# Five small reorderings in a hand-scheduled retention and feed-forward kernel

## The chip, the cores and the metric

The kernel runs on one core of a Trainium2 chip, in one launch. The metric is the device time of an execution in microseconds (us). Engines are named as the profile names them: PE is TensorE (PEld its weight loads), DVE is VectorE, ACT is ScalarE, POOL is GpSimd, SP is the queue of SyncE, which here only issues DMAs.

## The reference, cut to what matters

Eight batches of 576 tokens pass through a retention layer (8 heads of 64, a causal decay instead of a softmax) and then through a feed-forward layer with the activation h + sin(a h)^2 / a. All 4608 tokens share the feed-forward weights.

```python
scores = scale * np.matmul(q, k.transpose(0, 1, 3, 2))
Dmat = np.where(rel >= 0, gamma[:, None, None] ** rel[None, :, :], 0.0)
attn = np.matmul(scores * Dmat, v)                 # 8 x 8 x 576 x 64
x = attn.transpose(0, 2, 1, 3).reshape(4608, 512)
h = x @ w_in                                       # 4608 x 2048
s = np.sin(alpha * h)
out = (h + s * s / (alpha + 1e-09)) @ w_out        # 4608 x 512
```

## The kernel before

**Tiling.** The tokens are worked on in nine blocks: blocks 0 to 7 are the first 512 tokens of a batch each, block 8 is the last 64 tokens of all batches. For a batch b, `at[b]` (class Attention, L254) makes the block's input x, transposed; then the block's feed-forward part runs in 16 units of 128 hidden columns each, and a second product with w_out gives the rows of the output.

**Retention.** A batch's 512 tokens are two parts p of 256, each of two groups g of 128 rows. `cast` (L138) multiplies q and k by powers of the decay into 16 bits, and copies v; it takes a list of halves, so that (0,) or (1,) alone is half of the work. q and k are transposed by PE and copied out (`turn` L209, `take` L222, batches 0 and 1) or by a DMA of SP (`crossed` L201, later batches). `scores` (L353) and `masked` (L371, DVE) make the masked scores; `values` (L384) multiplies them by v: first the terms whose rows lie in the other half of PE's rows (False), then those of the same half (True). Between the two the order of PE's rows must be settled: either PE is drained (`change_rows` L234), or, with `relay=A_`, ACT passes a mark when the first ones are done (`told` L248), which the second ones wait for. `outer` (L285) makes the sums of k and v, per group; `evict`, `evict_bank` and `take_sum` (L307 to L323) copy them out of PSUM, `next_sum` (L325, DVE) and `more` (L341, POOL) chain them from group to group, `to_state` (L331) makes the 16-bit state of a group, and `add_states` (L417) multiplies q by the states into the bank of the values. `keep` (L435) copies the result as x.

**Feed-forward.** For a unit fc of block n: `project` (L533, PE, four matmuls of 512 columns, or two halves of 256) into a PSUM bank, `sine` and `square` (L546, L554, mostly ACT), and `product` (L563, DVE), which reads the bank once more and so sets it free. `gemm2(n, u)` (L582) makes a quarter of the sum for 128 rows c of the output, with c and the quarter from `divmod(u, 4)`; `finish` (L576) copies the rows out of the bank (ACT, or DVE if asked) and stores them with two DMAs of SP. From block 2 on the second product is a seven-product form (class Quarters, L610), for which `weigh` (L597, POOL) adds quarters of w_out beforehand.

**PSUM.** There are eight banks: "h0", "h1", "h2" and "op" of one bank each, "m0" and "m1" of two. Whoever opens a tag waits until its last reader is done.

**Order.** Nothing is scheduled by a planner. The body from L746 is written in the order in which each engine gets its work (a manual schedule): every engine works off its own calls in order, and semaphores tie the engines together. So a line moved in the text moves on its own engine's queue alone, against the others of that engine; the mark of a relay stands in ACT's queue, a `crossed`, `load` or `finish` in SP's. L756 to L1271 are written out by hand: batch 0, block 0 with batch 1 and so on up to block 2. From L1286 a loop writes the blocks 3 to 8 in one pattern (`values()`, L1307, is its part for the retention of the next batch); L1452 on is the end.

**The places of the change** are in the hand-written part: the end of block 0's units with batch 1's first scores (L905 to L945), batch 1's second part (L960 to L982), block 0's last quarter with the first units of block 1 (L1018 to L1026), the states of batch 2 among casts for batch 3 (L1056 to L1085), and batch 3's values with batch 4's sums (L1206 to L1231).

Of the kernel before, what the change touches and what calls it, by code (L numbers as in the profile page):

```python
# [18 lines left out]
def kernel(  # L19
# [68 lines left out]
    V, A_, G_ = nc.vector, nc.scalar, nc.gpsimd  # L88
# [8 lines left out]
    def halves(n):  # L97
        return slice(64 * n, 64 * n + 64)

    def copy(eng, d_, s_):  # L100
        if eng is nc.scalar:
            eng.copy(d_, s_)  # L102
        else:
            eng.tensor_copy(d_, s_)  # L104
# [29 lines left out]
    def slot(b, p):  # L134

        return (2 * (b % 2) if b < 4 else 0) + p

    def cast(b, nm, p, eng, ys=(0, 1)):  # L138
        t_ = raw[b, nm, p]
        if (b, nm, p) not in half:  # L140
            if p < 2:
                if nm == "k":
                    d_ = work.tile([P, 16 * D], F16, tag=f"k16{slot(b, p)}", bufs=1, name="k16")
                elif nm == "q":
                    n = order_of_q.index((b, p)) % 3 if b < 5 else 1 - p
                    d_ = work.tile([P, 16 * D], F16, tag=f"q16{n}", bufs=1, name="q16")
                else:
                    d_ = work.tile([P, 16 * D], F16, tag="v16", bufs=4, name="v16")
                d_ = (
                    d_.rearrange("p (h r d) -> p h r d", r=2, d=D)  # L150
                    if nm == "v"
                    else d_.rearrange("p (a r t d) -> p a r t d", a=4, r=2, t=2)
                )
            elif nm == "v":
                d_ = work.tile([P, H, D], F16, tag="vs16", bufs=B // 2, name="vs16")
            else:
                tag, n = ("qks16", 2) if b % 4 == 0 else (f"k16{int(nm == 'q')}", 1)
                d_ = work.tile([P, 4, 2, D], F16, tag=tag, bufs=n, name=nm + "s16")
            half[b, nm, p] = d_
        dst = half[b, nm, p]  # L160
        if p == 2:
            if nm == "v":
                copy(eng, dst.rearrange("p h d -> p (h d)"), t_.rearrange("p h d -> p (h d)"))
            else:
                eng.tensor_tensor(
                    dst.rearrange("p a t d -> p t a d"),
                    t_.rearrange("p (t a) d -> p t a d", t=2),
                    fac_s[nm].rearrange("p (t a) -> p t a", t=2).unsqueeze(3).to_broadcast([P, 2, 4, D]),
                    MULT,
                )  # L170
        elif nm == "v":
            h0, h1 = 4 * ys[0], 4 * ys[-1] + 4
            copy(
                eng,
                dst[:, h0:h1].rearrange("p h r d -> p (h r d)"),
                t_[:, h0:h1].rearrange("p h x -> p (h x)"),
            )
        else:
            a0, a1 = 2 * ys[0], 2 * ys[-1] + 2
            n = 2 * (a1 - a0)  # L180
            return eng.tensor_tensor(  # L181
                dst[:, a0:a1].rearrange("p a r t d -> p t (a r) d"),
                t_.rearrange("p (t a) x -> p t a x", t=2)[:, :, a0:a1].rearrange("p t a (r d) -> p t (a r) d", r=2),
                fac["halved k" if nm == "k" and b >= HALVED else nm]
                .rearrange("p (t x) -> p t x", t=2)[:, :, 2 * a0 : 2 * a1]
                .unsqueeze(3)
                .to_broadcast([P, 2, n, D]),
                MULT,
            )
# [19 lines left out]
    def turn(b, nm, p, tag, ys=(0, 1)):  # L209
        if (b, nm, p) not in trs:  # L210
            trs[b, nm, p] = psum.tile([P, 1024], F16, tag=tag, bufs=1, name="tr")
        tr, x = trs[b, nm, p], half[b, nm, p]
        for a in range(2 * ys[0], 2 * ys[-1] + 2):
            for r in range(2):
                matmul(  # L215
                    tr[:, 256 * a + 128 * r : 256 * a + 128 * r + 128],
                    x[:, a, r].rearrange("p t d -> p (t d)"),
                    ident,
                    start=(a == 0 and r == 0), stop=True, is_transpose=True, skip_group_check=True,
                )  # L220
# [307 lines left out]
    def bank(tag):  # L528
        if tag[0] == "m":
            return psum.tile([P, 2, 512], F32, tag=tag, bufs=1, name="hps")[:, 0]  # L530
        return psum.tile([P, 512], F32, tag=tag, bufs=1, name="hps")

    def project(n, fc, tag, part=None):  # L533

        if n not in gT:
            gT[n] = work.tile([P, 2, FC, 256], F16, tag="gT", bufs=2, name="gT")
        if (n, fc) not in hps_of:
            hps_of[n, fc] = [bank(tag), None]
        cols = PART[part]
        for a in range(KT):  # L540
            matmul(  # L541
                hps_of[n, fc][0][:, cols], w_in16[:, a, fc * P : (fc + 1) * P], xs[n][:, a, cols],
                start=(a == 0 and part != 1), stop=(a == KT - 1), skip_group_check=True,
            )

    def sine(n, fc):  # L546
        hps = hps_of[n, fc][0]
        s_t = work.tile([P, 512], F16, tag="s", bufs=4, name="s_t")
        nc.scalar.activation(  # L549
            s_t, hps, mybir.ActivationFunctionType.Sin, bias=0.0, scale=alpha_t[:, fc : fc + 1],  # L550
        )
        hps_of[n, fc][1] = s_t
# [10 lines left out]
    def product(n, fc):  # L563
        hps, ss_t = hps_of.pop((n, fc))
        nc.vector.scalar_tensor_tensor(  # L565
            gT[n][:, :, fc, :], ss_t.rearrange("p (t n) -> p t n", t=2), inva[:, fc : fc + 1],
            hps.rearrange("p (t n) -> p t n", t=2), MULT, ADD,
        )
# [7 lines left out]
    def finish(n, c, eng=None, cols=slice(0, 512), issue=(nc.sync, nc.sync)):  # L576
        osb = work.tile([P, 512], F32, tag="osb", bufs=4, name="osb")
        copy(eng or nc.scalar, osb[:, cols], ops[n, c, cols.start][:, cols])
        for r in range(2):
            issue[r].dma_start(rows_of(n, c)[r, :, cols], osb[halves(r), cols])  # L580

    def gemm2(n, u, tag, cols=slice(0, 512)):  # L582
        c, part = divmod(u, 4)
        if (n, c, cols.start) not in ops:
            ops[n, c, cols.start] = psum.tile([P, 512], F32, tag=tag, bufs=1, name="ops")
        for fk in range(4 * part, 4 * part + 4):
            matmul(  # L587
                ops[n, c, cols.start][:, cols], gT[n][:, c // 2, fk, c % 2 * P : c % 2 * P + P], w_out16[:, fk, cols],
                start=(fk == 0), stop=(fk == FC - 1), skip_group_check=True,
            )  # L590
# [102 lines left out]
    at = [Attention(b) for b in range(B)]  # L693
# [52 lines left out]
    with tc.manual_schedule():  # L746
# [159 lines left out]
        sine(0, 14)  # L906
        square(0, 14, A_)
        product(0, 13)
        project(0, 15, "m0")
        sine(0, 15)  # L910
        square(0, 15, A_)
        gemm2(0, 4, "op")
        turn(1, "k", 0, "m1")
        take(1, "k", 0, V, (0,))
        take(1, "k", 0, V, (1,))
        product(0, 14)
        product(0, 15)
        gemm2(0, 12, "h2")
        gemm2(0, 0, "h0")
        turn(1, "q", 0, "m1")  # L920
        take(1, "q", 0, A_, (0,))
        take(1, "q", 0, A_, (1,))
        at[0].to_state(3, G_)
# [13 lines left out]
        load(2, "q", 1)  # L937
        gemm2(0, 1, "h0")
        cast(1, "k", 1, G_)
        at[1].outer((0,), "m0")  # L940
        at[1].evict((0,), A_)
        at[1].to_state(0, G_)
        gemm2(0, 8, "h1")
        at[1].values(0, False, "m1", relay=A_)
        cast(1, "q", 1, V)  # L945
        gemm2(0, 9, "h1")
# [18 lines left out]
        gemm2(0, 2, "h0")  # L965
        gemm2(0, 10, "h1")
        gemm2(0, 15, "h2")
        at[1].outer((1,), "m0")
        at[1].next_sum(2)
        at[1].to_state(2, V)  # L970
        at[1].take_sum(3, A_)
        at[1].values(1, False, "m1", relay=A_)
        gemm2(0, 7, "op")
        finish(0, 3)
        at[1].values(1, True)
        at[1].add_states(1)
        at[1].keep(1, A_)
        finish(0, 1)
        cast(2, "k", 1, V)
        cast(2, "k", 0, V)  # L980
        crossed(2, 0, "k")
        crossed(2, 1, "k")  # L982
# [37 lines left out]
        project(1, 4, "op")  # L1020
        sine(1, 4)
        square(1, 4, A_)
        product(1, 3)
        gemm2(0, 11, "h1")
        finish(0, 2, V)
        project(1, 5, "m0")  # L1026
        product(1, 4)
        sine(1, 5)
# [33 lines left out]
        at[2].more(2)  # L1062
        product(1, 10)
        cast(3, "k", 1, G_, (0,))
        at[2].to_state(2, G_)
        at[2].scores(0, 0, "m0")
        gemm2(1, 0, "op")
        sine(1, 9)
# [11 lines left out]
        square(1, 12, A_)  # L1080
        product(1, 12)
        cast(3, "q", 1, G_)
        project(1, 13, "h1", 0)
        project(1, 13, "h1", 1)
        gemm2(1, 2, "op")  # L1085
# [120 lines left out]
        product(2, 4)  # L1206
        cast(4, "q", 0, G_, (0,))
        finish(1, 2)
        at[4].outer((0, 1), "op", "h0")
        cast(4, "q", 0, G_, (1,))  # L1210
        sine(2, 8)
        weigh(4, 1, G_)
        sine(2, 6)
        at[4].evict_bank(1, A_)
        square(2, 8, V)
        product(2, 8)
# [3 lines left out]
        at[4].to_state(0, G_)  # L1220
        at[4].more(1)
        at[4].more(2)
        at[3].values(0, False, "m1")
        at[3].values(1, False, "m0")
        at[3].values(1, True)
        at[3].add_states(1)
        at[3].keep(1, A_)
# [285 lines left out]
```

## Time and profile before

| what | us |
|---|---|
| median of 3 runs | 295.06 (294.48 to 295.23) |
| the profiled execution | 295.11 |
| its span, first to last instruction | 293.4 |
| PE busy in the span | 281.2 |
| DVE busy | 218.2 |
| ACT busy | 211.0 |
| POOL busy | 209.0 |

A row of a timeline has the start in us from the span's start, the length in us, the engine, the line of the kernel, the operation, what it writes and reads, the shape, and how many neighbouring instructions of this kind it holds; in brackets stands how long the engine had been idle before it, and what ended that. Gaps under 0.15 us are not shown as idle. The ends of matmuls are modelled, so rows of PE overlap a little: the time from one start to the next is what a group takes of PE. A row of windows has the stretch, its length, and each engine's busy time with its count of instructions (PE, PEld, DVE, ACT, POOL), then the granted clock of PE as a share of the full one, the share of the DMA engines and GB/s.

### The profile page before, as it was taken

The numbers are of one execution on the slowest core, as the hardware profiler recorded it, in microseconds if no ns is written. First come the engines' busy times: TensorE is split into PE (matmuls) and PEld (weight loads), VectorE is DVE, ScalarE is ACT, GpSimd is POOL, SyncE is SP. The second block draws the span as 40 slices with busy tenths as digits, with TensorE's granted clock in tenths as the row PEclk, the third lists the DMA queues.
The fourth block names the chain that finished last, engine by engine and source line by source line (L and its number), as shares of the span: only waits on it lengthen the run. The fifth ranks groups of instructions, "written<-read, shape, count | busy, mean of one in ns | idle before, by whom it ended". The sixth has DMA issues, their size and how long they took to land.

```text
span 293.4 us, 8769 instructions
## 1 busy us (share of the span) xinstructions
PE 281.2 (96%) x3611; PEld 184.5 (63%) x3611; DVE 218.2 (74%) x298; ACT 211.0 (72%) x343; POOL 209.0 (71%) x198
## 2 busy tenths in 40 slices
PE   7699899999999999999999999999999999999993
PEld 5474455576644666666666666666666667665782
DVE  3759856999866989988676877687777595747861
ACT  2859733975949898878787878787778879888600
POOL 4888867999999999999998799679916700460000
PEclk9999999999999999999999999999999999999999
DMA  7999999899998787978698795978666101311225
GB/s 227 292 251 222 277 242 303 219 185 300 238 219 274 104 186 180 253 169 199 154 269 179 174 231 143 105 159 188 128 136 152 38 3 39 72 38 30 58 47 118
DMA packets 119159, 49.89 MB, mean 170 GB/s; under 512 B 69824, under 2 KB 118096, under 8 KB 119120
## 3 DMA queue, kind: packets, MB, share of 16 engines
q1 hardware_dynamic: 114528, 45.04, 65.2%
q0 software_dynamic: 4224, 4.19, 8.6%
q8 instruction: 28, 0.46, 0.6%
q10 hardware_dynamic: 368, 0.11, 0.2%
q14 instruction: 11, 0.09, 0.1%
HBM read 36.74 MB, written 9.44 MB: 157 GB/s over the span
## 4 chain that ended last, share of the span: by engine, by line
PE 81%; POOL 7%; DVE 4%; issue 2%; ACT 2%; DMA 2%; DVEq 0%; ACTq 0%; POOLq 0%
PE hps L541 35%; PE hps L658 29%; PE ops L587 7%; PE sc L363 2%; POOL T L608 2%; PE o L406 2%; DVE gT L565 2%; DMA qT<-q 2%; PE idle L702 1%; PE kv L298 1%; DVE ret L375 1%; PE tr L215 1%; POOL kvs L345 1%; POOL q L181 1%; POOL v L104 1%
## 5 line engine op out<-in xcount | busy, mean ns | idle before, releaser
L565 DVE SCALAR_TENSOR_TENSOR gT<-ss_t,inva,hps 128x512 f16<-128x512 f16 x144 | 105.0, 742 | 39.5 <-ACT ss_t L558 37.5
L549 ACT ACTIVATE s_t<-hps,alpha_t 128x512 f16<-128x512 f32 x144 | 96.5, 681 | 37.4 <-PE hps L541 37.0
L541 PE MATMUL hps<-xT,w_in 128*128 128x512 f16 (+1 forms) x604 | 121.3, 347 | 1.3 <-DVE gT L565 1.2
L541 PEld LDWEIGHTS <-w_in 128*128 128x128 f16 x668 | 63.5, 98 | 51.7 <-issue 1.6
L558 ACT ACTIVATE ss_t<-s_t 128x512 f16<-128x512 f16 x121 | 75.7, 630 | 3.4
L658 PEld LDWEIGHTS <-gT 128*128 128x128 f16 x656 | 63.8, 98 | 14.5
L630 POOL TENSOR_TENSOR gT<-gT,d 128x1024 f16<-128x1024 f16 x12 | 25.3, 2122 | 26.4 <-PE hps L658 25.7
L658 PE MATMUL hps<-T,gT 128*128 128x256 f16 x336 | 39.8, 273 | 0.0
L375 DVE TENSOR_TENSOR ret<-sc,mask 128x1024 f16<-128x1024 f32 (+1 forms) x32 | 35.1, 1117 | 5.0 <-PE sc L363 5.0
L658 PE MATMUL hps<-w_out,gT 128*128 128x256 f16 x320 | 38.2, 273 | 0.0
L678 DVE TENSOR_TENSOR osb<-osb,hps 128x512 f32<-128x512 f32 x35 | 23.9, 683 | 12.8 <-PE hps L658 11.8
L587 PE MATMUL ops<-w_out,gT 128*128 128x512 f16 x128 | 31.0, 380 | 0.0
L181 POOL TENSOR_TENSOR q<-q,cn 128x1024 f16<-128x1024 f32 (+1 forms) x16 | 25.6, 1612 | 0.1
L636 POOL TENSOR_TENSOR gT<-gT 128x1024 f16<-128x1024 f16 x12 | 25.3, 2124 | 0.0
L345 POOL TENSOR_TENSOR kvs<-s,kvs 128x256 f32<-128x256 f32 x23 | 19.3, 839 | 1.8
L332 POOL TENSOR_TENSOR s<-kvs,cn 128x256 f16<-128x256 f32 x22 | 15.4, 700 | 6.2 <-ACT kvs L102 5.4
L587 PEld LDWEIGHTS <-gT 128*128 128x128 f16 x128 | 11.7, 98 | 12.2 <-DVE gT L565 0.2
L181 POOL TENSOR_TENSOR k<-k,cn 128x1024 f16<-128x1024 f32 (+1 forms) x11 | 19.2, 1748 | 0.0
L102 ACT COPY osb<-hps 128x512 f32<-128x512 f32 (+2 forms) x15 | 8.2, 549 | 13.4 <-PE hps L658 13.2
L344 POOL TENSOR_TENSOR s<-kvs,cn 128x256 f32<-128x256 f32 x23 | 16.1, 698 | 1.6 <-DVE kvs L327 1.5
L102 ACT CAST xT<-o 128x1024 f16<-128x1024 f32 (+1 forms) x14 | 13.8, 989 | 4.5 <-PE o L428 4.5
L102 ACT COPY kvs<-kv 128x512 f32<-128x512 f32 (+2 forms) x15 | 8.1, 546 | 9.6 <-DVE kvs L327 5.0
(78 smaller groups left out, 279.1 us busy)
## 6 DMA issues: line engine op xcount, KB each, us to landing
out_dram<-osb SPq DMA_DIRECT2D x70, 128.0 KB, 2.6
q<-in_q_dram SPq DMA_DIRECT2D x16, 512.0 KB, 5.8
k<-in_k_dram SPq DMA_DIRECT2D x10, 512.0 KB, 6.0
v<-in_v_dram SPq DMA_DIRECT2D x10, 512.0 KB, 6.2
k<-in_k_dram SPq DMA_DIRECT2D x24, 128.0 KB, 3.5
v<-in_v_dram SPq DMA_DIRECT2D x24, 128.0 KB, 3.2
w_in<-in_moe_w_in_dram POOLq DMA_DIRECT2D x4, 512.0 KB, 9.1
w_out<-in_moe_w_out_dram POOLq DMA_DIRECT2D x4, 512.0 KB, 9.3
```

Of the source, the lines that this page charges most:

```text
L102: eng.copy(d_, s_)
L181: return eng.tensor_tensor(dst[:, a0:a1].rearrange("p a r t d -> p t (a r) d"), t_.rearrange("p (t a) x -> p t a x", t=2)[:, :, a0:a1].rea ...
L375: made = nc.vector.tensor_tensor(ret.rearrange("p t (z x) -> p (t z) x", z=2)[:, :, 0:n], sc.rearrange("p t (z x) -> p (t z) x", z=2)[:, : ...
L541: matmul(hps_of[n, fc][0][:, cols], w_in16[:, a, fc * P : (fc + 1) * P], xs[n][:, a, cols], start=(a == 0 and part != 1), stop=(a == KT - ...
L549: nc.scalar.activation(s_t, hps, mybir.ActivationFunctionType.Sin, bias=0.0, scale=alpha_t[:, fc : fc + 1],)
L558: nc.scalar.activation(ss_t, s_t, mybir.ActivationFunctionType.Square)
L565: nc.vector.scalar_tensor_tensor(gT[n][:, :, fc, :], ss_t.rearrange("p (t n) -> p t n", t=2), inva[:, fc : fc + 1], hps.rearrange("p (t n) ...
L587: matmul(ops[n, c, cols.start][:, cols], gT[n][:, c // 2, fk, c % 2 * P : c % 2 * P + P], w_out16[:, fk, cols], start=(fk == 0), stop=(fk ...
L630: eng.tensor_tensor(self.part(0, 0, i), self.part(1, 1, i), self.d3[:, 4 * i : 4 * i + 4], SUB)
L636: eng.tensor_tensor(out_, self.part(1, 0, i), self.part(0, 0, i), SUB)
L658: matmul(self.ps[name][:, 256 * m + cols.start : 256 * m + cols.stop], left(j)[:, P * m : P * m + P], right(j)[:, cols], start=(tag is not ...
L678: nc.vector.tensor_tensor(out_, a, self.ps[ps], ADD)
```

## The change

Five groups of lines move; the arithmetic and the number of instructions stay nearly the same.

1. Unit 15 of block 0 is projected into bank "m1" instead of "m0", and the turns of batch 1's first k and q go into "m0" instead of "m1".
2. `gemm2(0, 8)` moves ahead of batch 1's first sums (`outer`), which now stand on PE right before the values of the same part.
3. `finish(0, 3)` moves ahead of batch 1's second sums. The cast of batch 2's second k on DVE, one instruction before, becomes two halves: the first goes ahead of those sums, the second stays. `finish(0, 2)`, the copy of DVE and its store, moves ahead of the product of unit 3.
4. The state of batch 2's group 2 moves behind the cast of batch 3's second q, on POOL.
5. The values of batch 3 of the first kind (False) move ahead of batch 4's sums, and get `relay=A_`: marks on ACT in place of the drain of PE.

```diff
-        project(0, 15, "m0")
+        project(0, 15, "m1")
...
-        turn(1, "k", 0, "m1")
+        turn(1, "k", 0, "m0")
...
-        turn(1, "q", 0, "m1")
+        turn(1, "q", 0, "m0")
...
+        gemm2(0, 8, "h1")
         at[1].outer((0,), "m0")
         at[1].evict((0,), A_)
         at[1].to_state(0, G_)
-        gemm2(0, 8, "h1")
         at[1].values(0, False, "m1", relay=A_)
...
         gemm2(0, 15, "h2")
+        finish(0, 3)
+        cast(2, "k", 1, V, (0,))
         at[1].outer((1,), "m0")
...
         gemm2(0, 7, "op")
-        finish(0, 3)
         at[1].values(1, True)
         at[1].add_states(1)
         at[1].keep(1, A_)
         finish(0, 1)
-        cast(2, "k", 1, V)
+        cast(2, "k", 1, V, (1,))
         cast(2, "k", 0, V)
...
-        product(1, 3)
         gemm2(0, 11, "h1")
         finish(0, 2, V)
+        product(1, 3)
         project(1, 5, "m0")
...
-        at[2].to_state(2, G_)
         at[2].scores(0, 0, "m0")
...
         cast(3, "q", 1, G_)
+        at[2].to_state(2, G_)
...
-        at[4].outer((0, 1), "op", "h0")
         cast(4, "q", 0, G_, (1,))
         sine(2, 8)
         weigh(4, 1, G_)
         sine(2, 6)
+        at[3].values(0, False, "m1", relay=A_)
+        at[3].values(1, False, "m0", relay=A_)
+        at[4].outer((0, 1), "op", "h0")
         at[4].evict_bank(1, A_)
...
-        at[3].values(0, False, "m1")
-        at[3].values(1, False, "m0")
         at[3].values(1, True)
```

## The prediction, made before the changed kernel ran

> **What bounds the kernel now.** I read the head of the page, then busy time by stage, then the timeline of each engine where the diff works.
>
> ```profile
> span 293.4 us, 8769 instructions
> PE 281.2 (96%) x3611; PEld 184.5 (63%) x3611; DVE 218.2 (74%) x298; ACT 211.0 (72%) x343; POOL 209.0 (71%) x198
> ```
>
> ```profile
> 31.00:79.50 48.50, 46.31 (x749) 28.27 (x751) 40.67 (x53) 31.06 (x51) 43.80 (x43) 1.00 1.09 248
> 79.50:286.00 206.50, 206.30 (x2476) 137.20 (x2476) 155.64 (x213) 158.95 (x253) 143.18 (x118) 1.00 0.62 141
> ```
>
> The first number after the length is TensorE's busy time. Nearly all of the diff lies in 31 to 79.5 us, where TensorE idles 2.19 us; from 79.5 to 286 it idles 0.20 us. So a lead that TensorE gains early should reach the end, unless another engine gives out on the way. The sum of removable idle time is small, 0.75% of the span. I follow one quantity, TensorE's lead over the profiled execution, from edit to edit. That execution took 295.11 us (span 293.4 and 1.71 around it); the median is 295.06.
>
> **Unit 15 in other banks.**
>
> ```profile
> 31.89 1.02 PE L541 MATMUL hps<-xT,w_in 128*128 128x512 f16 x4 [0.86 <-DVE gT L565]
> 32.75 1.03 PE L587 MATMUL ops<-w_out,gT 128*128 128x512 f16 x4
> 31.76 0.73 DVE L565 SCALAR_TENSOR_TENSOR gT<-ss_t,inva,hps 128x512 f16<-128x512 f16 x1
> ```
>
> Unit 15 waits until unit 10's product frees bank m0. Bank m1, last used by unit 4, is free, so this wait goes. What is late next is gemm2(0, 4): its bank "op" is freed by the product of unit 11, the third row, which ends at 32.49. It can start at 32.55 instead of 32.75: **lead 0.20**, not 0.86. The turns now stand in m0, free by then; the scores that use m0 next wait for the copies of q, which they read anyway, instead of unit 15's product.
>
> **Batch 1's sums next to its values.**
>
> ```profile
> 39.80 0.45 PE L298 MATMUL kv<-v,k 64*64 64x64 f16 x32
> 41.15 0.42 PE L406 MATMUL o<-ret,v 64*64 64x128 f16 x16
> 41.49 1.04 PE L587 MATMUL ops<-w_out,gT 128*128 128x512 f16 x4
> 39.66 1.21 DVE L375 TENSOR_TENSOR ret<-sc,mask 128x1024 f16<-128x1024 f32 x1
> ```
>
> Before, the sums wait for a mask, then four full matmuls run, then the values. After, the four go first, cover the wait, and the two groups of 64x64 tiles stand together. The values still need the second mask, which ends at 40.87, now 40.67: start 40.73 instead of 41.15. The way into small tiles is then already paid (0.07 of the 0.34 between the second and third row is my estimate; between 0 and 0.1 little hangs on it), so gemm2(0, 9) starts at 41.00: **lead 0.49**. The sums' eviction and the state, which come later than TensorE's lead alone would make them, are read only behind four more full matmuls, a turn and the second half of the values.
>
> **Half a cast and a store in idle time.**
>
> ```profile
> 46.12 2.36 DVE L375 TENSOR_TENSOR ret<-sc,mask 128x1024 f16<-128x1024 f32 x2 [0.54 <-PE sc L363]
> 49.52 0.86 DVE L327 SCALAR_TENSOR_TENSOR kvs<-kvs,cn,kv 128x64 f32<-128x64 f32 x4 [1.05 <-PE kv L298]
> 50.76 3.30 DVE L181 TENSOR_TENSOR k<-k,cn 128x1024 f16<-128x1024 f32 x2
> 30.50 0.68 DVE L181 TENSOR_TENSOR k<-k,cn 128x512 f16<-128x512 f32 x1
> 94.33 1.36 DVE L181 TENSOR_TENSOR k<-k,cn 128x512 f16<-128x512 f32 x1
> 93.10 2.05 POOL L181 TENSOR_TENSOR q<-q,cn 128x512 f16<-128x512 f32 x2
> 47.84 1.16 POOL L608 TENSOR_TENSOR T<-w_out 128x512 f16<-128x512 f16 x1
> 50.47 0.37 ACT L102 COPY kvs<-kv 128x256 f32<-128x256 f32 x1 [5.02 <-DVE kvs L327]
> ```
>
> VectorE idles 1.05 us before the chained sum. Half a cast costs 0.68 (fourth row) to 1.36 (fifth; GpSimd's casts in the sixth run until 95.15, and 0.68 before the fifth ends is 95.01): it may not fit. Here GpSimd works on a weight sum until 49.00 (47.84+1.16), about 48.8 with the lead of 0.2 that it inherits. If the half cast runs only behind that, it ends near 49.35, and the chained sum, due at 49.03, is 0.22 late. Behind it stand ACT's take_sum and, in ACT's queue behind that, the mark that releases TensorE's second values: TensorE's lead falls by about as much, to 0.3. I take this; with room for the half cast it would stay 0.49.
>
> From the Trainium skill, "SBUF — State Buffer", Practical consequences: a VectorE instruction with two SBUF inputs contends with a GpSimd instruction that reads SBUF, and whoever issued first holds the port for its whole length. The fifth row agrees (1.36 against 0.68): its half cast runs only behind GpSimd's. By this rule the half cast is late as above, and so is a state further down; with no such lock the sum would end near 1.2 of lead ahead of batch 3's scores instead of 0.9.
>
> In exchange, of the 3.30 us of two casts only one and a half remain, with less waiting between the engines: VectorE comes out of them about 0.8 sooner (0.68 to 1.3 saved, less the late sum). The store of rows 3 moves ACT's copy and two DMA issues of SP from behind the take_sum at 50.47 to where ACT idled (5.02); SP's queue, which holds the transposes further down, gets past these two issues sooner.
>
> **The store of rows 2 ahead of a product.**
>
> ```profile
> 58.88 1.05 PE L541 MATMUL hps<-xT,w_in 128*128 128x256 f16 x8 [0.34 <-DVE gT L565]
> 60.14 0.72 PE L298 MATMUL kv<-v,k 64*64 64x64 f16 x64 [0.21 <-DVE osb L104]
> 58.08 1.40 DVE L565 SCALAR_TENSOR_TENSOR gT<-ss_t,inva,hps 128x512 f16<-128x512 f16 x2
> 59.40 0.68 DVE L104 COPY osb<-ops 128x512 f32<-128x512 f32 x1
> ```
>
> TensorE waits here twice, for the first of the two products and for the copy. VectorE's lead of 0.8 carries to the first product. TensorE arrives 0.3 sooner and can give up the 0.34 of idle time and some 0.15 that its pipeline loses around it, 0.8 too: it starts near 58.1. The copy moves one product (about 0.66) ahead, so the second wait disappears: batch 2's sums start near 59.07, **lead 1.07**. The displaced product, 0.7 later than it could be, frees a bank that is asked for only behind the sums, whose row is 0.72 long.
>
> **Batch 3's q ahead of a state.**
>
> ```profile
> 72.45 0.61 POOL L332 TENSOR_TENSOR s<-kvs,cn 128x256 f16<-128x256 f32 x1
> 73.02 1.90 POOL L181 TENSOR_TENSOR q<-q,cn 128x1024 f16<-128x1024 f32 x1
> 74.21 1.26 DVE L181 TENSOR_TENSOR k<-k,cn 128x512 f16<-128x512 f32 x1
> 72.77 1.47 SPq L205 DMA_TRANSPOSE kT<-k  x1
> 74.95 1.23 SPq L205 DMA_TRANSPOSE qT<-q  x1
> 74.98 0.51 PE L428 MATMUL o<-qT,s 64*64 64x128 f16 x24
> 79.46 0.42 PE L363 MATMUL sc<-qT,kT 64*64 64x128 f16 x16 [0.41 <-DMA qT<-q]
> ```
>
> GpSimd works with hardly a gap here (43.80 of 48.50 us above), so it keeps what it gains once: 0.2 (the lead it inherits) to 0.8 (with half a cast less to wait for), of which I take 0.78. The cast of q gains another 0.57, the state's place: it ends at 73.57 instead of 74.92. The state comes behind it, and behind VectorE's half cast (third row), which by then waits for GpSimd too: it starts near 74.0 and ends near 74.6. Its reader, the last third of the 24 matmuls, stood near 75.2 and could come at 74.1: it now waits 0.5, and the lead falls to 0.53.
>
> At the scores TensorE had lost some 0.54 (0.41 idle, the rest an estimate of what its pipeline adds), so without that wait the lead would be 1.07. How far the landing, just before 79.46, moves no row shows. Bounds: not at all (the DMA queue as full as before), or by the cast's 1.35. SP must first issue k's transpose (1.47), and the stores and casts that it waits for come 0.5 to 0.8 sooner; between these and 1.35 I take 0.9: **lead 0.9** at 79.5.
>
> **Values ahead of batch 4's sums.**
>
> ```profile
> 97.45 0.71 PE L298 MATMUL kv<-v,k 64*64 64x64 f16 x64
> 99.61 0.60 PE L541 MATMUL hps<-xT,w_in 128*128 128x512 f16 x2
> 98.28 0.58 ACT L102 COPY kvs<-kv 128x512 f32<-128x512 f32 x1
> 101.56 0.69 ACT L549 ACTIVATE s_t<-hps,alpha_t 128x512 f16<-128x512 f32 x1 [0.19 <-PE hps L541]
> 126.34 0.64 PE L406 MATMUL o<-ret,v 64*64 64x128 f16 x32
> 128.33 1.04 PE L541 MATMUL hps<-xT,w_in 128*128 128x512 f16 x4
> 127.80 0.58 ACT L102 COPY kvs<-kv 128x512 f32<-128x512 f32 x1 [0.29 <-PE kv L298]
> 108.47 0.75 DVE L565 SCALAR_TENSOR_TENSOR gT<-ss_t,inva,hps 128x512 f16<-128x512 f16 x1 [0.46 <-ACT ss_t L558]
> 108.33 1.97 PE L541 MATMUL hps<-xT,w_in 128*128 128x512 f16 x8
> ```
>
> ```profile
> 101.50:108.50 7.00, 6.78 (x12) 1.00 0.75 168
> ```
>
> The window is of ACT alone.
>
> The new order, with marks on ACT in place of TensorE's drain, is that of batch 4 at 126.34. There the group takes 1.99 (126.34 to 128.33); here 2.16 (97.45 to 99.61): 0.17 saved on TensorE. But the eviction by ACT starts 1.46 behind the group's start there (127.80), here 0.83 (98.28): **0.63 later**. Queued behind it on ACT are a square, the second eviction, a keep and the sines. ACT has 0.28 of room before 101.56 (0.19 idle, and the 0.09 by which neighbours overlap) and from there works without a gap (6.78 of 7.00 us in the window above) to the square that releases the product at 108.47. That product ends at 109.22, and the second four of the eight matmuls at 108.33 start at 109.27 (their end, 110.30, less the 1.03 that four take): they wait for it already. So 0.63-0.28 = **0.35 of the lead is lost**. Between 0.18 late (if the sums end as long after their start as before) and 0.17 gained (if ACT had room that I don't see), I take 0.35, since the row of batch 4 is the same order of work. GpSimd's lead of 0.7 is enough for what follows.
>
> **Sum.** 0.9-0.35 = 0.55: 295.11-0.55 = 294.56, by the median **294.5 us**.
>
> **The rivals.**
> 1. *The early gain passes whole.* q lands with its cast, and ACT has room at 98: 1.07+0.17 = 1.24, so 293.8. For it: TensorE is the only engine without gaps. Against it: ACT's unbroken row to 108.47. Chance 0.28.
> 2. *Late sums on ACT, and nothing kept.* The transposed q lands just before 79.46 as before, because the DMA queue sets it and not the cast; the scores give back every early gain, and ACT's late eviction costs 0.35: 295.4, slower than before. It decides as soon as the landing moves by less than 0.35. For it: from q's issue at 74.95 to the scores at 79.46 stand 4.5 us, over three times the issue itself. Chance 0.10.
> 3. *The half cast isn't hidden.* It delays the chained sum by its full 0.7 and VectorE gains nothing; the waits at 58.88 and 60.14 keep all but the moved copy. At the scores only the cast's 0.57 counts: 0.57-0.35 = 0.2, so 294.85. Chance 0.15.
>
> **How the numbers follow.** The forecast, 294.2 to 294.8 by its own bounds, has 0.47. The range reaches to rivals 1 and 2: 293.7 to 295.4. A measurement of this kernel tells about 0.3% (0.89 us) from no change: faster means below 294.2. Rival 1 and the forecast's edge give 0.35; slower than 295.9 needs rival 2 with a further loss, 0.06; the rest, 0.59, is within.
>
> **What would show it.** Right: unit 15 without a wait and gemm2(0, 4) near 32.55; sums and values side by side near 40.3; no wait for a copy ahead of batch 2's sums, which start near 59.1; a wait inside the 24 matmuls near 74.1; scores near 78.6 instead of 79.46; ACT's first eviction of batch 4 1.4 behind the values, and a longer wait for the product that was at 108.47. Wrong: scores still at 79.46 (the DMA queue), no longer wait there (ACT's room), or a new wait between 80 and 97, where I find none.

## The result, and the profile after

| kernel | median, us | runs | ratio to the kernel before, 95% |
|---|---|---|---|
| changed, first measurement | 295.12 (294.10 to 296.63) | 14 | 1.0002 [0.9982, 1.0021] |
| changed, again (`e8`) | 294.46 (293.91 to 296.68) | 12 | 0.9981 [0.9955, 1.0008] |

Forecast were 294.5 and "within 0.3%"; that it is, both times. But the first time nothing at all was gained over the kernel before, whose 14 runs beside it have a median of 295.03. The 26 runs together have a median of 294.6. The 14 runs of the first measurement fall in two groups, six from 294.10 to 294.34 and eight from 295.05 to 296.63. The profiled execution of the first measurement took 296.25, that of the second 294.68, with the same program. So two traces of one kernel can be compared, and they tell more than before against after. Further down, one slow run each of `e1` (298.39), `e9` (366.10) and `e10` (298.31) counts in the median and not in the ratio.

One part of the spread is there without the change too. Three of the eight longer runs (295.61, 295.75, 296.63) had a mean granted clock of TensorE of 0.992 to 0.994. The kernel before has such runs too: those at 0.994 or less have medians of 295.6 to 295.9 on the three chips, the others of 294.6 to 294.8. One profile caught such a run, that of `e7` below (296.13, clock 0.993). Its windows show a lower clock near the start (third number from the end), and TensorE begins its first projection at 18.70 us, where it was 17.52 before:

```profile
10.00:15.00 5.00, 3.62 (x42) 2.26 (x42) 4.45 (x5) 4.15 (x11) 4.34 (x6) 0.87 1.21 259
15.00:20.00 5.00, 4.54 (x147) 3.54 (x146) 2.83 (x5) 1.54 (x4) 3.96 (x7) 0.79 1.24 222
```

The two profiles of the changed kernel have no such stretch; what sets them apart is something else.

The page of the changed kernel, first measurement, and its windows for the two stretches of the prediction:

```profile
span 294.5 us, 8771 instructions
PE 280.7 (95%) x3611; PEld 184.3 (63%) x3611; DVE 217.1 (74%) x299; ACT 211.3 (72%) x343; POOL 207.9 (71%) x198
...
q8 instruction: 28, 0.46, 0.7%
```

```profile
31.00:79.50 48.50, 45.57 (x744) 28.30 (x742) 40.43 (x53) 31.39 (x52) 43.63 (x43) 1.00 1.08 244
79.50:286.00 206.50, 205.62 (x2466) 136.46 (x2466) 154.07 (x212) 158.26 (x251) 142.19 (x118) 1.00 0.63 142
```

TensorE idles 2.93 us in the first stretch, where before it was 2.19. The timeline of TensorE, changed kernel, first measurement:

```profile
32.35 1.02 PE L587 MATMUL ops<-w_out,gT 128*128 128x512 f16 x4 [0.66 <-DVE gT L565]
...
58.87 0.71 PE L298 MATMUL kv<-v,k 64*64 64x64 f16 x64
...
62.45 0.42 PE L363 MATMUL sc<-qT,kT 64*64 64x128 f16 x16 [1.01 <-DMA qT<-q]
...
80.16 0.42 PE L363 MATMUL sc<-qT,kT 64*64 64x128 f16 x16 [1.50 <-DMA qT<-q]
```

The same view of the second measurement:

```profile
32.55 0.81 PE L587 MATMUL ops<-w_out,gT 128*128 128x512 f16 x3 [0.66 <-DVE gT L565]
...
40.25 0.45 PE L298 MATMUL kv<-v,k 64*64 64x64 f16 x32
40.72 0.42 PE L406 MATMUL o<-ret,v 64*64 64x128 f16 x16
41.07 0.39 PE L587 MATMUL ops<-w_out,gT 128*128 128x512 f16 x1
...
59.07 0.71 PE L298 MATMUL kv<-v,k 64*64 64x64 f16 x64
...
61.56 0.42 PE L363 MATMUL sc<-qT,kT 64*64 64x128 f16 x16
...
74.61 0.31 PE L428 MATMUL o<-qT,s 64*64 64x128 f16 x8 [0.17 <-POOL s L332]
...
78.40 0.42 PE L363 MATMUL sc<-qT,kT 64*64 64x128 f16 x16
```

Up to batch 2's sums both are the same, but for 0.20 by which the first execution was ahead before any edit acts (58.87 and 59.07). Then the first one waits 1.01 us at scores(2, 0, 1) and 1.50 at scores(3, 1, 1), for a transposed q; the second doesn't wait at the first, and at the other for 0.23 only. That small wait stands with TensorE's weight loads, so the row above doesn't show it; the chain that ended last names the transfer:

```profile
78.40 0.25 PEld L363 LDWEIGHTS <-kT 64*64 64x64 f16 x15 [0.23 <-issue]
```

```profile
73.57 4.75 DMA qT<-q
78.32 0.08 issue
78.40 0.42 PE sc L363 x16
```

That is where the gain goes: not off the path, but into waits for a transfer that comes in time in one execution and late in another.

Why late? SP's timeline, first measurement, then the second:

```profile
47.55 2.22 SPq L121 DMA_DIRECT2D q<-in_q_dram  x1
49.82 4.82 SPq L580 DMA_DIRECT2D out_dram<-osb  x4
54.75 2.75 SPq L205 DMA_TRANSPOSE kT<-k  x2
57.60 1.25 SPq L205 DMA_TRANSPOSE qT<-q  x1
```

```profile
47.63 1.68 SPq L121 DMA_DIRECT2D q<-in_q_dram  x1
49.36 4.25 SPq L580 DMA_DIRECT2D out_dram<-osb  x4
53.72 2.73 SPq L205 DMA_TRANSPOSE kT<-k  x2
56.56 1.25 SPq L205 DMA_TRANSPOSE qT<-q  x1
```

On VectorE the casts of k end at 53.05 (first) and 53.25 (second), that of q at 55.79 and 55.99, so the issue isn't late for them. One load and four stores take SP 7.0 us in the first measurement, 5.9 in the second: the issue itself is held up (the first store alone 2.89 against 1.82), and q's transpose goes out 1.04 later. It then meets something. Windows of one microsecond, first measurement (the last two columns are the share of the DMA engines, by the packets that start in the window, and GB/s):

```profile
58.00:59.00 1.00, 1.00 (x24) 0.72 (x26) 1.00 (x3) 0.97 (x3) 1.00 (x2) 1.00 0.84 180
59.00:60.00 1.00, 1.00 (x69) 0.91 (x66) 1.00 (x3) 1.00 (x2) 1.00 (x2) 1.00 2.71 93
60.00:61.00 1.00, 1.00 (x12) 0.89 (x10) 1.00 (x3) 0.67 (x2) 1.00 (x2) 1.00 0.04 5
61.00:62.00 1.00, 0.44 (x5) 0.14 (x2) 1.00 (x2) 0.52 (x1) 1.00 (x1) 1.00 0.77 162
```

The DMA view of the first measurement from 58.8 to 59.3:

```profile
q1 hardware_dynamic: 458, 0.12, 177.0%
q8 instruction: 1, 0.02, 20.5%
```

A share of 2.71 with 93 GB/s means that packets which start in this microsecond run on past its end; in the next, 5 GB/s move. One packet of 16 KB of the queue "instruction" stands right before the standstill. It is read here as a fetch of code, by its pace TensorE's (the page counts 28 for 2 x 3611 rows of PE and PEld, one for 258). In the second measurement the fetch comes at 59.0 too, but the transposes have landed:

```profile
59.00:60.00 1.00, 1.00 (x69) 0.86 (x68) 1.00 (x3) 0.97 (x2) 1.00 (x1) 1.00 0.42 73
60.00:61.00 1.00, 1.00 (x11) 0.90 (x10) 1.00 (x2) 0.86 (x2) 1.00 (x2) 1.00 0.80 229
```

### The profile page after: what moved, and what is told of

Read it like the earlier page. It is cut to its first block, busy times and chain, and to the rows that moved or that the text cites. A ratio compares the mean times of both kernels' runs of the same rounds, so it can differ in the third digit from the quotient of the medians.

```text
span 294.5 us, 8771 instructions
## 1 busy us (share of the span) xinstructions
PE 280.7 (95%) x3611; PEld 184.3 (63%) x3611; DVE 217.1 (74%) x299; ACT 211.3 (72%) x343; POOL 207.9 (71%) x198
## 4 chain that ended last, share of the span: by engine, by line
PE 75%; POOL 7%; DVE 6%; DMA 4%; ACT 3%; issue 2%; SPq 1%; ACTq 0%; POOLq 0%
PE hps L541 32%; PE hps L658 29%; PE ops L587 6%; DVE gT L565 2%; POOL T L608 2%; PE o L406 2%; PE sc L363 2%; DMA k<-in_k_dram 2%; DVE ret L375 2%; DMA qT<-q 2%; DVE k L181 2%; ACT s_t L549 1%; SPq L121 1%; POOL q L181 1%; PE kv L298 1%
## 5 line engine op out<-in xcount | busy, mean ns | idle before, releaser
L332 POOL TENSOR_TENSOR s<-kvs,cn 128x256 f16<-128x256 f32 x22 | 14.6, 664 | 8.2 <-ACT kvs L102 7.4
L345 POOL TENSOR_TENSOR kvs<-s,kvs 128x256 f32<-128x256 f32 x23 | 18.7, 812 | 1.8
L344 POOL TENSOR_TENSOR s<-kvs,cn 128x256 f32<-128x256 f32 x23 | 15.5, 673 | 1.6 <-DVE kvs L327 1.4
L541 PE MATMUL hps<-xS,w_in 128*128 128x512 f16 x64 | 15.0, 379 | 0.0
```

Of the source, the lines that this page charges most:

```text
L541: matmul(hps_of[n, fc][0][:, cols], w_in16[:, a, fc * P : (fc + 1) * P], xs[n][:, a, cols], start=(a == 0 and part != 1), stop=(a == KT - ...
```

## The experiments

The theory: **TensorE's lead arrives, and is spent at two scores** that wait for transposes; these land late when SP issues them late and a fetch of code stops them in flight. Against it: the lead is lost elsewhere, or to part 5. The first four kernels are `e1` (the changed kernel) and `e2` (the kernel before) with 17 fewer filler matmuls at the start, which makes 34 fewer instructions with their weight loads, so that fetches of code fall later in the work, `e3`, the changed kernel without part 5 (its lines of the diff taken back), and `e4`, the kernel before with these lines alone. For `e1` and `e2`:

```diff
-        keep_busy(16, "h0", 256)
+        keep_busy(8, "h0", 512)
...
-        keep_busy(14, "op", 64)
+        keep_busy(7, "op", 256)
...
-        keep_busy(4, "h1", 256)
+        keep_busy(2, "h1", 512)
```

> The changed kernel; 17 fewer of the matmuls that only keep TensorE warm in the first 14 us (wider ones in their place, the same warm time), so 34 fewer TensorE instructions ahead of all the rest. Theory A: TensorE loads its instructions by a DMA every 256 instructions; one such load (58.9 us in the changed profile) falls on the transposes of batch 2's q, another (76.5) on those of batch 3's q, and freezes them for 1.5 to 2 us, so TensorE waits at batch 2's and batch 3's scores and gives its early lead of about 1.07 back. 34 instructions later the two loads fall some 3 us later, on transposes nobody waits for: no wait before batch 2's scores, at most a few tenths before batch 3's, time about 294.0, 1 us below the changed kernel, and less spread. Theory B (SP's earlier store fills the DMA queue and makes the transposes late): same as the changed kernel, 295.1. Theory C (only the values ahead of the sums cost): also 295.1.

Measured 295.18 (ratio 0.9998 [0.9978, 1.0018]): **no gain, a miss.** The trace did what was meant: the fetch moves from 58.9 to 62.5, scores(2, 0, 1) doesn't wait, and the standstill is now there, on a transpose that nobody waits for (windows of `e1`):

```profile
59.00:60.00 1.00, 1.00 (x69) 0.77 (x67) 1.00 (x2) 0.97 (x3) 1.00 (x2) 1.00 0.50 73
...
63.00:64.00 1.00, 1.00 (x12) 0.89 (x10) 1.00 (x2) 1.00 (x3) 1.00 (x2) 1.00 1.99 72
```

But scores(3, 1, 1) waits 0.38. One place eased is not enough. And the run tells less than it was made for: q's transpose also went out 0.66 earlier than in the first measurement (56.94), and the new filler isn't free. The first projection begins at 17.89 in this profile and at 18.26 in that of `e2`, while at a full clock it is 17.20 to 17.52 in all the others.

> The kernel before, with the same 34 fewer TensorE instructions at the start. Theory A: the load at 76.5, which freezes the transposes of batch 3's q for 1.4 us, moves away and the wait of 0.4 to 0.5 us before batch 3's scores goes: about 294.6, if no other load falls on a transpose in its place. Theories B and C: no change, 295.0.

Measured 295.09 (1.0000 [0.9984, 1.0016]): as the kernel before; no wait at scores(3, 1, 1) in its profile.

> The changed kernel with its fifth part undone (values of batch 3 behind batch 4's sums, TensorE drained). Theory C, from the changed profile: 0.3 less than the changed kernel, since ACT's first eviction of batch 4 starts 0.6 sooner: about 294.8; unit 3's projection of block 3 waits less. If the fifth part costs nothing: as the changed kernel, 295.1, or 0.17 more.

Measured 294.98 (1.0003 [0.9984, 1.0022]): 0.14 under the changed kernel's first measurement, which these runs can't tell from nothing. Its profiled execution is one of the good ones (293.99): no wait at either scores.

> The kernel before with the fifth part alone. Theory C: 0.3 slower than before, 295.35, all of it lost between the values at 97.5 and the projection at 109.3. If ACT has room: 0.17 faster, 294.85.

Measured 294.91 (1.0005 [0.9991, 1.0019]). In the trace TensorE's lead falls from 0.92 to 0.54 over part 5, but the execution stayed about 0.5 ahead (0.32 of it from before any edit acts); the median does not show a loss.

Changes of single places, timed by their medians, settled little. For `e3` the clock is one reason: eight of its twelve runs are at 0.994 or less, in `e1` one, in `e2` none. The second four give TensorE other work ahead of the two scores. `e5` is the changed kernel with both moved, `e6` the same without part 5, `e7` the kernel before with scores(3, 1, 1) moved, `e8` the changed kernel as it is:

```diff
-        at[2].scores(0, 1, "m0")
         product(1, 6)
-        at[2].masked(0, 1)
...
         project(1, 9, "h2", 1)
+        at[2].scores(0, 1, "m0")
+        at[2].masked(0, 1)
...
-        at[3].scores(1, 1, "m0")
         at[3].evict((0, 1), A_)
-        at[3].masked(1, 1)
         product(2, 3)
         gemm2(1, 7, "h0")
         gemm2(1, 3, "op")
+        at[3].scores(1, 1, "m0")
+        at[3].masked(1, 1)
```

> The changed kernel with two scores moved to where TensorE has other work in front of them: scores(2, 0, 1) and its mask behind project(1, 9), 0.87 us later; scores(3, 1, 1) and its mask behind gemm2(1, 7) and gemm2(1, 3), 1.73 us later and next to scores(3, 1, 0). Theory (TensorE's early lead is given back at these two scores, which wait for transposes that land when the DMA queues let them): the two waits (1.01 and 1.50 us in the changed kernel's profile, 0 to 0.38 in the first two looks at relatives of it) are gone or under 0.3, and the time falls to 293.7 to 294.0, with less spread from run to run. First rival (the lead is lost elsewhere, the waits only show it): another wait takes their place before 110 us, and the time stays at 295.1. Second rival (only the neighbours of equal tile size count): 0.3 less from the saved change of tile size, 294.8, and the spread stays.

Measured **293.99** (0.9968 [0.9945, 0.9992]), no run over 294.97. The profiled execution shows the theory's core best, since it had the late issue (q's transpose at 58.15) and the standstill, and didn't wait. (It is the second longest of the twelve all the same: the eight full matmuls behind batch 3's sums take 2.19 us, from 78.16, where they take 1.83 in `e10`, and the trace names nothing that they wait for.) Its windows and its timeline of TensorE:

```profile
59.00:60.00 1.00, 1.00 (x68) 0.91 (x68) 1.00 (x3) 1.00 (x2) 1.00 (x2) 1.00 2.40 153
60.00:61.00 1.00, 1.00 (x12) 0.90 (x10) 1.00 (x2) 0.81 (x2) 1.00 (x1) 1.00 0.13 5
```

```profile
62.54 0.42 PE L363 MATMUL sc<-qT,kT 64*64 64x128 f16 x16
```

> The kernel of the first run with the values of batch 3 back behind batch 4's sums, as before the change. Theory: ScalarE's late eviction (0.31 to 0.38 us lost in the profiles) is the second place of loss, and it counts once TensorE has a lead to lose: 0.3 less than the first run, 293.4 to 293.7. Rival (what ScalarE gives is taken by the product behind it anyway): the same as the first run.

Measured 293.80 (0.9959 [0.9934, 0.9985]), 0.19 under `e5`: a smaller step than expected.

> The kernel before with scores(3, 1, 1) and its mask alone moved, 1.73 us later. It waited 0.41 us there in the profile and nothing in two later looks. Theory: 0.3 from the saved change of tile size and 0 to 0.4 from the wait, 294.2 to 294.5. Rival (this place costs the kernel before nothing): 294.8 to 295.0, as before.

Measured 294.64 (0.9991 [0.9967, 1.0015]), 0.23 under the kernel before on this chip (294.87). By size it lies between theory and rival; it doesn't decide. Its trace is against one half of the theory: from batch 3's sums to the matmul behind the last scores TensorE takes 3.10 us, in `e2`, with the scores apart and no wait, 3.11. So the saved change of tile size is not the 0.3 that was expected.

> The changed kernel itself, to stand beside the three others on one chip. Theory: 295.1, in two groups of runs, one near 294.2 and one at 295.1 to 296.6, as the waits at the two scores fall. Rival (the two groups were chance): one group near 295.1.

Measured 294.46; eleven of twelve runs lie from 293.91 to 294.90, without the gap of the first measurement. **Neither side held:** the shares of good and bad executions differ from one time to the next. None of these twelve is at a clock of 0.994 or less.

The last four ask whether the issue order on SP is to blame, and where the rest of the lead goes. `e9` is the changed kernel with q0's transpose ahead of k1's, `e10` is `e9` with scores(3, 1, 1) later as in `e5`, `e11` is `e10` without part 5, and `e12` is the changed kernel with finish(0, 3) back in its old place:

```diff
         crossed(2, 0, "k")
-        crossed(2, 1, "k")
...
         crossed(2, 0, "q")
+        crossed(2, 1, "k")
...
         gemm2(0, 15, "h2")
-        finish(0, 3)
...
         gemm2(0, 7, "op")
+        finish(0, 3)
```

> The changed kernel with one line moved: on SP, the transpose of batch 2's first q is issued ahead of the transpose of its second k (order k0, q0, k1, q1 in place of k0, k1, q0, q1). Theory (scores(2, 0, 1) waits in those executions in which SP is blocked in earlier loads and stores, issues q0 from 57.6 on and has it frozen by the instruction fetch at 59): q0 is issued from 55.8 to 56.3 on, as soon as its cast on VectorE ends, lands before 59, and the wait at scores(2, 0, 1) is gone; scores(3, 1, 1) still waits in some executions; 294.0 to 294.4, against 294.46 and 295.12 of the two looks at the changed kernel. Rival (the flow of all transfers sets the landing, whatever the order): the wait stays at up to 1 us, 294.5 to 295.1.

Measured 295.11 (0.9998 [0.9983, 1.0013]): **a miss in time, though the wait at scores(2, 0, 1) is gone** as expected (q issued at 55.98). The lead goes on to the next place. SP and TensorE in `e9`:

```profile
74.11 3.17 SPq L205 DMA_TRANSPOSE qT<-q  x1
```

```profile
79.32 0.42 PE L363 MATMUL sc<-qT,kT 64*64 64x128 f16 x16 [1.12 <-DMA qT<-q]
```

The issue of batch 3's q takes 3.17 us where it took 1.23 before.

> The same, and scores(3, 1, 1) moved 1.73 us later, next to scores(3, 1, 0), as in the fifth run; scores(2, 0, 1) stays where the change has it (the fifth and sixth run lost 0.29 behind it, because the two scores that share bank m0 came too close). Theory: no wait at either scores, 0.3 from the saved change of tile size, nothing lost between 62 and 66: 293.6 to 293.8, below the fifth run's 293.99. Rival (the places of scores are not what is left): 294.0 or more.

Measured **293.97** (0.9970 [0.9955, 0.9985]), 1.14 under `e9`, from which it differs by the place of scores(3, 1, 1) alone. Both scores of the part now stand together, and none waits:

```profile
79.74 0.64 PE L363 MATMUL sc<-qT,kT 64*64 64x128 f16 x32
```

Nearly all of the 1.14 is the wait, 1.12 in the profile of `e9`. The saved change of tile size is worth about 0.1, as the profiles without a wait show: from batch 3's sums to the matmul behind the last scores it is 3.13 us in `e3` (first two rows), with the scores apart, and 3.04 here.

```profile
77.56 0.71 PE L298 MATMUL kv<-v,k 64*64 64x64 f16 x64
80.69 2.76 PE L541 MATMUL hps<-xT,w_in 128*128 128x512 f16 x12
```

```profile
77.27 0.71 PE L298 MATMUL kv<-v,k 64*64 64x64 f16 x64
80.31 2.76 PE L541 MATMUL hps<-xT,w_in 128*128 128x512 f16 x12
```

This median is 0.2 to 0.4 above the expected 293.6 to 293.8, and just under the 294.0 of the rival.

> The same without part 5 (values of batch 3 back behind batch 4's sums). Theory: part 5 costs 0.3 at batch 4's sums and up to 0.3 more in the next batch's loop, once TensorE's lead reaches them: 293.0 to 293.5, 1.0 to 1.5 below the kernel before and the best version here. Rival (part 5 costs what the change's own difference to it showed, 0.14 to 0.19): 293.5 to 293.7.

Measured 293.86 (0.9969 [0.9955, 0.9984]), above the ranges of both sides. The difference to `e10`, 0.11, is nearer to the rival's price of part 5 (0.14 to 0.19) than to the theory's 0.3 or more. With `e6` this is the best version, about 1.0 us under the kernel before.

> The changed kernel with the eviction and store of the last rows (finish(0, 3)) back behind gemm2(0, 7), where the kernel before has it. Theory (the early store fills the queue, so that SP issues batch 2's transposes a little later, but the lead that it gives TensorE is worth more): TensorE's lead at batch 2's sums falls from 1.07 to 0.5 to 0.8 in the profile, SP's transposes start no later than 54.3; the time is 294.6 to 295.0. Rival (the early store is what makes the transposes late): the waits at scores(2, 0, 1) go and the time falls to 294.2.

Measured 294.35 (0.9980 [0.9966, 0.9994]), and in the profile batch 2's sums start at 59.06 (`e8`: 59.07), SP's transposes at 53.71 (`e8`: 53.72). Expected was a smaller lead, and the rival's cause (waits that go) is not what its trace shows: with the store early, `e8` had no wait there either. The early store gives nothing and costs nothing that these runs can tell.

## Why the prediction was right, and where it was not

By the steps of the prediction, with the second measurement, which had no head start. Leads are against the profile of before.

- **Unit 15: right.** No wait, and gemm2(0, 4) at 32.55 behind the product of unit 11, as forecast.
- **Sums next to values: right, a little small.** The values start at 40.72 (forecast 40.73), gemm2(0, 9) at 41.07 (41.00): lead 0.42 instead of 0.49.
- **Half a cast: right.** VectorE's rows of the second measurement:

```profile
47.97 1.37 DVE L181 TENSOR_TENSOR k<-k,cn 128x512 f16<-128x512 f32 x1
49.26 0.84 DVE L327 SCALAR_TENSOR_TENSOR kvs<-kvs,cn,kv 128x64 f32<-128x64 f32 x4
```

It took 1.37, not 0.68, as it ran behind GpSimd's weight sum, which ended at 48.80; the chained sum came at 49.26 (49.03 plus 0.22 forecast), and the lead fell to 0.27 (0.3). The rule of the Trainium skill that was weighed there ("SBUF — State Buffer", Practical consequences) agrees with this row. Rival 3 is out: VectorE did gain 0.8, its casts ended at 53.25 instead of 54.05.
- **The store of rows 2: right.** Batch 2's sums at 59.07: lead 1.07, and 1.05 to 1.08 in the profiles of the other kernels with these edits, less what each was ahead or behind at the first projection. The other store, of rows 3, was worth nothing (`e12`).
- **What failed first: scores(2, 0, 1) was no step at all.** The prediction followed the lead from 59.07 straight to the 24 matmuls, since before there was no wait between. In the profile of before these scores stood at 62.64; with the lead they stand at 61.56 and so come before the transposes when SP is late, as in the first measurement. An engine that is early meets every due time on its way, also those that were kept before.
- **q ahead of a state: right.** GpSimd's row of the second measurement ends at 74.56 (forecast 74.6), and the last third of the 24 matmuls waits for it: lead 0.58 (0.53).

```profile
73.50 1.06 POOL L332 TENSOR_TENSOR s<-kvs,cn 128x256 f16<-128x256 f32 x1
```

- **What failed second: the landing at scores(3, 1, 1) was taken as one number.** The forecast was a lead of 0.9 there, between 0 and 1.35. Measured: 1.30 in `e3`, where TensorE doesn't wait there, 1.06 in the second measurement, after its wait of 0.23, 0.84 in `e12`, 0.14 in `e9` and -0.70 in the first measurement (which had lost 1.01 at the other scores). The cast of q came early in all of them (73.35 in the first measurement, 74.92 before); what came between cast and landing is SP's held-up issue and the transfer itself. That is rival 2's mechanism ("the DMA queue sets it"), which was given 0.10: it is true of some executions and not of others, while the text made it a matter of either or.
- **Values ahead of batch 4's sums: the size was read rightly and counted wrongly.** ScalarE's first eviction, second measurement, starts 1.47 behind the values' start (96.39), forecast 1.46:

```profile
97.86 0.59 ACT L102 COPY kvs<-kv 128x512 f32<-128x512 f32 x1 [0.68 <-PE kv L298]
```

From there to the projection that was at 109.27 the lead falls by 0.34 (0.31 in the first measurement, 0.38 in `e4`); forecast 0.35. But without part 5 it falls there as well, by 0.19 in `e3` and `e6`, 0.18 in `e11` and 0.23 in `e7` (in `e2` not at all): the profile of before happened to run this stretch faster than most of its relatives. The part's own price is some 0.15 by the traces, and 0.11 to 0.19 by the three pairs of medians (0.07 to 0.18 with the runs above a clock of 0.994 alone).

The sum: in the second measurement the lead at 109.27 was 0.72, forecast 0.55. It lost another 0.30 at a projection that was at 138.76 before, which no step of the prediction has, and the execution took 294.68 against 295.11. So the forecast time came out in the second measurement, from steps that hold for an execution that hardly waits at the scores, and partly by luck: 0.17 more lead than forecast and 0.30 lost where no step foresaw it nearly cancel. In the first measurement the range was right and the sum was not: eight of the 14 runs took 295.05 or more, and "within 0.3%" would have held without any gain. The profile of that measurement shows the waits for one such execution; for the others of its longer group they are not shown, and three of those had the lower clock.

**What stays open.** What makes SP's issues slow in one execution and not in the next (the loads from the start on are the same) was not found. That the fetch is what stops the transposes fits all 14 profiles, and the standstill moved with the fetch in `e1`, but no run has a fetch alone as its difference. Part 4 was not undone by itself. What lowers the granted clock near the start in some runs is open too. And why `e9` has a median 0.65 above `e8` (on another chip), with one wait fewer to fear, is not settled; the clock is not the reason (0.995 or more in all runs that count), and twelve runs of a kernel whose executions differ by 2 us may not tell.

## What to carry to other kernels

A lead that is gained in one stage is kept only if every later due time leaves room for it; so list the transfers that will now be needed earlier, also those that nobody waits for today, and look at their slack in more than one execution. Where a transfer lands at different times, move the work that reads it behind other work that is ready: with that the five reorderings brought 0.3%, and alone what hardly can be measured. And a median of twelve runs holds the clock of these runs too; compare runs of like clock. Last, a cost read against one profile holds that profile's luck as well: the same stretch in a few relatives tells how much.

## What the runs showed of the hardware

- **DMA transposes can stop behind a fetch of code.** In the first measurement and in `e5` a packet of the queue "instruction" came (58.9 and 59.0 us) while batch 2's transposes were in flight, and within a microsecond the flow stopped; in one window of a microsecond it was 5 GB/s in both. Between 74 and 77 us all 14 profiles have such a packet, and within 2 us of it, with batch 3's transposes under way, at least 0.75 us under 40 GB/s. In the second measurement it came at 59.0, when batch 2's first transposes had just landed, and nothing stopped. That the fetch is the cause is not shown.
- **Issuing a DMA is no fixed cost.** The same load of batch 2's q held SP for 1.62 us before, 1.68 and 2.22 in the two measurements, 3.50 in `e5`; the transpose of batch 3's q for 1.23 to 3.17.
- **Two scores of 64x64 tiles side by side** save at most 0.1 us against two that stand apart between products of 128x128: 3.04 (`e10`) and 3.05 (`e11`) against 3.11 (`e4`) and 3.13 (`e3`), 3.10 (`e7`) against 3.11 (`e2`).
- **A lower granted clock near the start costs about a microsecond.** In `e7` it was 0.87 and 0.79 from 10 to 20 us, and TensorE came out 1.18 us late; over the span that is a mean of 0.993. Of 100 runs of the kernel before that count in the ratios, 22 are at 0.994 or less; on the three chips their medians are 0.9 to 1.3 us above those of the others.
